# Attention with a gated feed-forward block on one core: the second weight block is converted during attention, the magnitude of the next raw words is taken ahead of the sigmoid, and scale chains move

## The chip, the core and the metric

The kernel runs on one core of a Trainium2 chip. Its time is the device time of one execution in microseconds (us); three timed runs of the kernel before gave 844.94, 845.30 and 847.82 us, median 845.3. Engines are named as in the profile: PE (matrix products), PEld (its weight loads), DVE (VectorE), ACT (ScalarE), POOL (GpSimd), SP (the queue from which most DMAs are issued; ACT and POOL issue some too).

## The reference

```python
# q, k, v: (4, 12, 448, 64); w_pre, w_post: (12, 12)
scores = scale * q @ k^T
scores = einsum('bhij,hg->bgij', scores, w_pre)      # heads mixed before the softmax
attn = softmax(scores, axis=-1)
attn = einsum('bhij,hg->bgij', attn, w_post)         # heads mixed after it
x = (attn @ v), heads side by side                   # 1792 tokens x 768
xn = x / sqrt(mean(x * x) + 1e-6) * rms_g
g, val = xn @ w_gate, xn @ w_val                     # 768 -> 1536 each
out = (g * sigmoid(g) * val) @ w_out                 # 1536 -> 768
```

The three feed-forward weights arrive as 64-bit floating point numbers; the kernel turns each into 32-bit ones by bit operations, then into a pair of fp16 tiles (a high part and a remainder).

## The kernel before, in words

**Attention.** Each of the four batches is cut into four chunks of 120 query rows (the last is shorter), and a chunk into 6, 6, 6 or 5 steps: 92 steps in all, numbered t. A step runs on every engine in turn: PE makes scores of a later chunk (`qk`), mixes heads (`sp`), and of the step before mixes again (`pm`) and multiplies with v (`av`); DVE takes the row maximum (`nm`, L193), copies (`st` L158, `at_all` L240), and makes reciprocals (`t`, `rp`); ACT takes the exponential; POOL scales the second mixing matrix (`wn`). Every engine works off its own list in order. What else stands in a step is put there by tables: `jobs_at[t]` at the head of step t, `last_at[t]` at its end. `first_w` is such a job: it converts the weights of the feed-forward block 0 in four pieces of 384 columns, seven steps a piece, one instruction a step on DVE for the first five, then a store to DRAM (`wf`) and a sum of magnitudes on ACT. `fetch_w` loads a piece. The chains (`first_w_ops`, `x_scale_ops`) find one power-of-two scale from such sums: some 12 tiny DVE instructions each, two or more a step, all through one small tile `square`.

**Feed-forward.** There are 12 blocks f of 128 gate and 128 value columns, and in each the four batches b. For one (f, b) PE makes 36 products of 128x448 (`pg`, then `pv`; `both` L703 to L705 in the first row, `product` L711 to L713 later), and `swiglu` follows on DVE (`sg` L755, `u` L758), ACT (the sigmoid form `Silu`, L756) and POOL (L759). The product tiles are six PSUM tiles, three pairs. Block 0 is done in `first_row`, block 1 to 11 in the loop after it, then comes the product with w_out (`po`, 756 products).

**Converting a block.** A block has two halves of 768 columns (gate, value); `load_w` gives each three steps: `fetch` (a 768 KB DMA into `wraw`, two buffers), `begin` (ACT: the magnitude of the upper raw words, L561), `half` (DVE: four instructions L535 to L538, which need that magnitude) with its tail (ACT: sum of magnitudes, L576). `even` then runs a scale chain on DVE and writes the fp16 pair: `wh` on ACT (L929), `wl` on DVE (L933). In `convert` the magnitude stands right before the four DVE instructions. In blocks f = 2, 3, 5, 6, 8, 9 two halves of w_out are converted beside the next block's (`queue_out`); in f = 4, 7, 10 `scale_out` runs one more chain and scales four tiles on ACT.

**First row.** `first_row` converts block 1 from raw words: two loads on the ACT queue, one half ahead of the scale chain of batch 3 (`x_scale_ops(3)`, L637 to L639) and of its `x_split` (hi on ACT L673, lo on DVE L674, two of six lo on POOL L671), one after `swiglu` of batch 1, then `even(1)` with its chain. `last_rms(0)` sums columns (`pss`, L323) and ends in the tile `d`, which `spread(3)` (`psy`, L373) needs on PE after the first product of block 1.

Of the kernel before, what the change touches and what calls it, by code (L numbers as in the profile page):

```python
# [10 lines left out]
I32 = mybir.dt.int32  # L11
# [38 lines left out]
def attention_moe(ctx: ExitStack, tc, q, k, v, wpre, wpost, mask, ident, wgv, wo, rms_g, out):  # L50
# [5 lines left out]

    const = pool(ctx, "const")
    dram = ctx.enter_context(tc.tile_pool(name="dram", bufs=1, space=bass.MemoryType.DRAM))
    wf = [dram.tile([128, KT * 128], F32, name=f"wf{p}") for p in range(2)]
    xd = [dram.tile([128, KT, SP_], F32, name=f"xd{b}") for b in range(B)]  # L60
    td = [[dram.tile([128, KT, S], F32, name=f"td{i}_{g}") for g in range(2)] for i in range(7)]

# [334 lines left out]
    def job(t, f, *a):  # L397
        jobs_at[t].append((f, *a))

    for n in range(NCHUNK):  # L400
        b, c = divmod(n, NC)
        if n > 2:
            for i in range(2):
                job(6 * n - 16 + 3 * i, load_q, n, 3 * i, 3, nc.sync)
        for hp in range(H // 2):
            if n == 0:
                job(5 + 2 * hp, load_v, 0, heads_of(0)[hp])
        if n == 4:
            for i in range(4 * 7):
                job(first[n] + 4 + i, lambda i: first_w(i), i)  # L410
            for p in range(4):
                job(first[n] + 7 * p, lambda p: fetch_w(p), p)
    for t, todo_ in enumerate(list(qk_at)):
        for n, hp in todo_:
            if n % NC == NC - 1 and n + 1 < NCHUNK:
# [12 lines left out]
            op()  # L428

    chain(16, lambda: gain_ops(), 2)  # L430
    chain(first[4] + 34, lambda: first_w_ops(), 2)
    for b in range(B - 1):
        t = first[NC * b + NC + 2] + (5 if b < B - 2 else 3)
        for i in range(17):
# [150 lines left out]
    def w_pair(pl):  # L585
        return [pl.tile([128, 2 * FT, 128], F16, name=f"w{n}", tag=f"w{n}")[:, :FT] for n in "hl"]
# [29 lines left out]
            op()  # L616
        return o[:, 1:2], o[:, 2:3]

    stats = const.tile([128, 72], F32, name="stats")
    g_scale, w_scale = stats[:, 52:], stats[:, 0:20]  # L620

    def gain_ops():
        o = g_scale[:, 4:7]
# [2 lines left out]
            lambda: nc.vector.tensor_scalar(gain, g_sb, o[:, 1:2], None, ALU.mult)  # L626
        ]

    def first_w_ops():
        unit[0] = w_scale[:, 18:19]  # L630
        return largest(w_scale, 4) + power(w_scale[:, 16:19], 2, g_scale[:, 6:7])

    def x_scale_ops(b):
        t = stats[:, 20 + 13 * (b % 2) :][:, :13] if b < 2 else const.tile([128, 13], F32, name=f"stat{b}")
        o, sc = t[:, 4:7], t[:, 7:13]
        scale_x[b] = sc, o[:, 2:3]
        first_ = lambda: nc.vector.tensor_reduce(t[:, :1], sums[b][:, :S], AX.X, ALU.max)  # L637
        return [first_] + largest(t, 1, X_LEAST, X_MOST) + power(o, -59, None, 24) + [
            lambda: nc.vector.tensor_scalar(sc, g_scale[:, 8:14], o[:, 1:2], None, ALU.mult)  # L639
        ]  # L640
# [88 lines left out]

    def fetch_w(p):  # L730
        raw = conv["raw", p] = pq.tile([128, 384, 2], I32, name="wraw", tag="wraw", bufs=3)
        src = wgv[0, :, 3 * p : 3 * p + 3].rearrange("p a f -> p (a f)").bitcast(I32)
        nc.sync.dma_start(raw.rearrange("p n t -> p (n t)"), src)

    def first_w(i):

        p, i = divmod(i, 7)
        if i < 5:
            if i == 0:
                conv["t"] = pq.tile([128, 2, 384], I32, name="wac", tag="wraw", bufs=3)  # L740
                conv[p] = to_f32(conv.pop(("raw", p)), *(conv["t"][:, j] for j in range(2)))
            conv[p][i]()
        elif i == 5:
            nc.sync.dma_start(wf[p // 2][:, (p % 2) * 384 : (p % 2) * 384 + 384], conv["t"][:, 1].bitcast(F32))
            junk = conv["t"].bitcast(F32)
            nc.scalar.activation(junk[:, 0], junk[:, 1], AF.Abs, scale=2.0 ** -12, accum_out=w_scale[:, p : p + 1])

    stores, first_ps, todo = [], [], []

# [39 lines left out]
    def start_b():  # L789
# [11 lines left out]
        def w_split(p):  # L801
            hi, lo = (t[:, 3 * p : 3 * p + 3] for t in w[0])
            f = raws.pop(("w", p)).rearrange("p (a f) -> p a f", f=128)
            up = w_scale[:, 17:18]
            nc.scalar.activation(hi, f, AF.Copy, scale=up)
            nc.vector.scalar_tensor_tensor(lo, f, up, hi, ALU.mult, ALU.subtract)

# [50 lines left out]
    def part_b(ps_p):  # L858
# [41 lines left out]
        def mix(o, x, y, op=ALU.subtract):  # L900
            nc.gpsimd.tensor_tensor(o, x, y, op)

        def fetch(eng=nc.sync):
            while work and len(fetched) < 2:
                fetched.append(work.pop(0))
                fetched[-1][0].fetch(fetched[-1][1], eng)

        def convert(f):
            if fetched and fetched[0][2] <= f:
                half, p, _ = fetched.pop(0)  # L910
                half.begin(p)
                return lambda: half(p)
            return lambda: lambda: None

        aged = []

# [38 lines left out]

        def first_row():

            queue(1)
            fetch(nc.scalar)
            for b in range(B - 1):  # L960
                spread(b)
            for b in range(1, B):
                first_ps.append([ps_p.tile([128, S], F32, name=n, tag="p") for n in ("pg", "pv")])
            for kk in range(KT):
                both(first_ps[1], w[0], xs[1], kk)
            swiglu(0, 0, *first_ps[0])
            raw3 = b_pools["narrow"].tile([128, 2 * KT, S], F32, name="raw3", tag="xn01")
            for p in range(3):
                nc.sync.dma_start(raw3[:, 2 * p : 2 * p + 2], xd[3][:, 2 * p : 2 * p + 2, :S])
            raws.update({(3, kk): raw3[:, kk] for kk in range(KT)})  # L970
            while todo:
                ahead()
                _, (f, *a), *_ = todo.pop(0)
                f(*a)
            for kk in range(KT):
                both(first_ps[2], w[0], xs[2], kk)
            convert(0)()()
            for op in x_scale_ops(3):
                op()
            for kk in range(KT):  # L980
                x_split(3, kk, nc.gpsimd if kk % 3 == 1 else nc.vector)
            swiglu(1, 0, *first_ps[1])
            convert(0)()()
            for kk in range(KT):
                both(first_ps[3], w[0], xs[3], kk)
            low = even(1)
            low(0)
            low(1)
            swiglu(2, 0, *first_ps[2])
            last_rms(0)  # L990
            small.extend(const.tile([128, SP_], F32, name=n, tag="sum", bufs=2) for n in ("small", "junk"))
# [11 lines left out]

        first_row()
        for f in range(1, FT - 1):
            queue(f + 1)
            if f in OUT_AT:
                queue_out(OUT_AT[f], f)
        for f in range(1, FT):
            for b in range(B):  # L1010
# [8 lines left out]
                even_next = f < FT - 1  # L1019
                product(pg, (hi[:, :KT], lo[:, :KT]), x)  # L1020
                product(pv, (hi[:, KT:], lo[:, KT:]), x)
                second = convert(f)
                if even_next and b == 2:
                    low = even(f + 1)
                if even_next and b == 3:
                    low(1)
                count()
                tail = second()
                if even_next and b == 2:
                    low(0)  # L1030
                if f == FT - 1:
# [5 lines left out]
                    h_load(3)  # L1037
                swiglu(b, f, pg, pv)
                tail()
                if f in SCALE_AT and b:  # L1040
                    for i in ((0, 1), (2,), (3,))[b - 1]:
                        scale_out(SCALE_AT[f], i)
                if f == 1 and b == 0:
                    last_rms(1)
                if f == FT - 1:
# [134 lines left out]
```

## Time and profile before

| what | value |
|---|---|
| median of three timed runs | 845.3 us |
| the profiled execution: device time, span | 850.1 us, 848.1 us |
| PE busy | 803.2 us, 95% |
| DVE, ACT, POOL busy | 615.1 us 73%, 509.4 us 60%, 343.7 us 41% |
| attention, up to the first product of batch 1 | 0 to 362.4 us |
| first row, up to block 1 | 362.4 to 392.4 us |
| blocks 1 to 11 | 392.4 to 701.3 us |
| product with w_out, then the last stores | 701.3 to 848.1 us |

The profiled execution is 4.8 us longer than the median. Its busy times are those of a whole run; what matters for the change is where PE stands still, since PE is busy in all but 5% of the span. A bracket at the end of a row of the timeline gives the engine's idle time before that instruction and what ended it. PE's rows overlap: a product of 448 columns is shown as 0.35 us, and the next begins 0.19 us after it. `PEclk` is the granted share of PE's clock: 1.00 is 2.4 GHz, 0.50 is 1.2 GHz.

### The profile page before, as it was taken

Reading aid. Unit: us, or ns where it says so; the run is one execution under the profiler, and the core shown is the slowest. Engines: PE = TensorE matmul, PEld = TensorE weight load, DVE = VectorE, ACT = ScalarE, POOL = GpSimd, SP = SyncE. Lnnn points to the kernel's source line nnn. Section 1 sums busy time; section 2 is a strip of 40 time slices with the busy share of each in tenths; the row PEclk is TensorE's granted clock in tenths of the full one; section 3 lists DMA queues with packets and bytes.
Section 4 is the critical chain, followed back from the end, with each engine's and each line's share of the span. In section 5 each row is a group of like instructions: output and inputs, shape, how many; then the busy total and the mean of one; then the engine's idle time right before and its main releaser. Section 6 shows DMA issues by size and latency. Waiting matters only on the chain.

```text
span 848.1 us, 27070 instructions
## 1 busy us (share of the span) xinstructions
PE 803.2 (95%) x10900; PEld 490.3 (58%) x10900; DVE 615.1 (73%) x1303; ACT 509.4 (60%) x1129; POOL 343.7 (41%) x469
## 2 busy tenths in 40 slices
PE   6998998999899999896999999999999999999998
PEld 2566777767777777643555555554554455555554
DVE  5776887787787767778687878787878776547661
ACT  3676777577767776763535354445353556869850
POOL 8112443354335346841442423324334357462210
PEclk9999999999999999998999999999999999999999
DMA  7677778666855654561545553644456246466641
GB/s 218 193 227 222 218 208 234 194 201 187 222 172 181 200 173 134 177 211 37 183 129 157 165 151 102 206 142 152 134 157 203 80 155 201 112 215 174 189 137 66
DMA packets 81087, 144.58 MB, mean 170 GB/s; under 512 B 10383, under 2 KB 72493, under 8 KB 80963
## 3 DMA queue, kind: packets, MB, share of 16 engines
q1 hardware_dynamic: 79166, 138.45, 54.9%
q0 software_dynamic: 832, 2.06, 1.0%
q10 hardware_dynamic: 965, 2.34, 0.8%
q8 instruction: 86, 1.41, 0.7%
q14 instruction: 38, 0.31, 0.1%
HBM read 72.04 MB, written 31.21 MB: 122 GB/s over the span
## 4 chain that ended last, share of the span: by engine, by line
PE 73%; DVE 12%; ACT 5%; issue 4%; DMA 2%; POOL 2%; ACTq 0%; SPq 0%; DVEq 0%; POOLq 0%
PE pm L227 10%; PE qk L138 9%; PE sp L186 8%; PE av L271 8%; PE po L711 6%; PE po L713 6%; PE po L712 6%; PE pg L713 4%; PE pg L711 3%; PE pg L712 3%; PE pv L712 3%; PE pv L711 3%; PE pv L713 3%; DVE sg L755 1%; DMA td<-keep 1%
## 5 line engine op out<-in xcount | busy, mean ns | idle before, releaser
L200 ACT ACTIVATE e<-sp,nm 128x448 f32<-128x448 f32 x180 | 114.2, 637 | 91.4 <-DVE nm L193 88.2
L186 PE MATMUL sp<-r,wk_pre 64*64 64x448 f32 x720 | 163.8, 542 | 3.8 <-issue 2.7
L138 PE MATMUL qk<-k,q 64*64 64x448 f32 x768 | 153.2, 557 | 7.7 <-DMA q<-in_q 4.2
L193 DVE TENSOR_REDUCE nm<-sp 128x1 f32<-128x448 f32 x180 | 111.0, 621 | 49.9 <-PE sp L186 25.2
L227 PEld LDWEIGHTS pm<-wn,e 60*64 60x64 f32 x5152 | 109.6, 134 | 47.9 <-POOL wn L212 25.2
L212 POOL TENSOR_SCALAR wn<-wk,rp 128x60 f32<-128x60 f32 x180 | 57.4, 333 | 192.7 <-DVE rp L209 127.7
L227 PE MATMUL pm<-wn,e 60*64 60x60 f32 x5152 | 109.9, 220 | 14.5 <-issue 11.5
L711 PE MATMUL pg<-x,wh 128*128 128x448 f16 x264 | 94.7, 359 | 9.2 <-ACT wh L929 9.2
L759 POOL TENSOR_TENSOR sg<-sg,u 128x448 f32<-128x448 f32 x36 | 43.9, 1220 | 145.2 <-ACT sg L756 135.5
L756 ACT ACTIVATE sg<-sg,unit 128x448 f32<-128x448 f32 x44 | 29.3, 667 | 121.0 <-DVE sg L755 121.0
L271 PE MATMUL av<-at_all,v 64*64 64x240 f32 (+4 forms) x1728 | 95.7, 321 | 3.1 <-issue 3.1
L713 PE MATMUL pg<-x,wl 128*128 128x448 f16 x264 | 94.4, 358 | 1.7 <-DVE wl L933 1.6
L712 PE MATMUL pg<-x,wh 128*128 128x448 f16 x264 | 94.5, 358 | 0.0
L711 PE MATMUL pv<-x,wh 128*128 128x448 f16 x264 | 93.0, 352 | 0.0
L712 PE MATMUL pv<-x,wh 128*128 128x448 f16 x264 | 93.0, 352 | 0.0
L713 PE MATMUL pv<-x,wl 128*128 128x448 f16 x264 | 93.0, 352 | 0.0
L713 PE MATMUL po<-h,fac 128*128 128x448 f16 x252 | 88.8, 352 | 0.0
L711 PE MATMUL po<-h,fac 128*128 128x448 f16 x252 | 88.8, 352 | 0.0
L712 PE MATMUL po<-h,fac 128*128 128x448 f16 x252 | 88.8, 352 | 0.0
L711 PEld LDWEIGHTS <-wh 128*128 128x128 f16 x528 | 51.9, 98 | 58.5 <-ACT wh L929 10.1
L713 PEld LDWEIGHTS <-wl 128*128 128x128 f16 x528 | 52.0, 98 | 52.5 <-DVE wl L933 3.8
L712 PEld LDWEIGHTS <-wh 128*128 128x128 f16 x528 | 52.0, 98 | 48.9 <-issue 1.6
(182 smaller groups left out, 1583.5 us busy)
## 6 DMA issues: line engine op xcount, KB each, us to landing
r<-st SPq DMA_DIRECT2D x117, 210.0 KB
hraw<-td SPq DMA_DIRECT2D x84, 224.0 KB
wraw<-in_wgv SPq DMA_DIRECT2D x20, 768.0 KB
td<-keep SPq DMA_DIRECT2D x48, 224.0 KB
wraw<-in_wo SPq DMA_DIRECT2D x12, 768.0 KB
r<-st SPq DMA_DIRECT2D x44, 175.0 KB
v<-in_v SPq DMA_DIRECT2D x24, 256.0 KB
k<-in_k SPq DMA_DIRECT2D x24, 224.0 KB
```

Of the source, the lines that this page charges most:

```text
L138: nc.tensor.matmul(ps[j][m, :S], qt[n][sl, hp, m], kt[n // NC, hp][sl], start=True, stop=True)
L186: nc.tensor.matmul(o, wk_pre[sl], rt[n][sl, 2 * p + v_], start=True, stop=True)
L193: nc.vector.tensor_reduce(t, ps[:, :S], AX.X, ALU.max, negate=True)
L200: nc.scalar.activation(e, ps[:, :S], AF.Exp, bias=nmx.pop((n, p, u)), accum_out=sm[n, p][:, u : u + 1])
L212: nc.gpsimd.tensor_scalar(wn[n, p][:, u], wk, r[:, u : u + 1], 1.0, ALU.mult, ALU.mult)
L227: nc.tensor.matmul(o[:, :, at_], e[u_][sl, j : j + JT], w_, start=True, stop=True)
L271: nc.tensor.matmul(x, vt[b, hp][sl, j, c_], a, start=(c_ == 0), stop=(c_ == JC - 1))
L711: nc.tensor.matmul(ps, a, xh[:, kk], start=(kk == 0), stop=False)
L712: nc.tensor.matmul(ps, a, xl_[:, kk], start=False, stop=False)
L713: nc.tensor.matmul(ps, a2, xh[:, kk], start=False, stop=(kk == KT - 1))
L756: nc.scalar.activation(sg, sg, AF.Silu, scale=unit[f])
L759: nc.gpsimd.tensor_tensor(h, sg, u, ALU.mult)
```

## The change

1. `first_w` and `fetch_w` now cover eight pieces, those of block 0 and of block 1 (`ROWS[p // 4]`): the four steps' lead of the load is kept, the conversions start four steps sooner (step 23) and run to step 78 instead of 54. Two more DRAM tiles `wf` hold the result.
2. The chain of block 0 starts at step 52 instead of 57; a second chain for block 1 runs from step 79, three instructions a step.
3. `first_row` no longer converts block 1 from raw words. It loads two finished 384 KB tiles on the ACT queue, writes `wh` (ACT) and `wl` (DVE) from them after the last split of batch 2, and only then runs `swiglu` of batch 0. The six lo parts of batch 3 are all on DVE. The loads of block 2 are issued ahead of these splits, and the first half of block 2 is converted after `swiglu` of batch 1.
4. In the loop `begin` is split from `convert`: the magnitude of the next half is issued after this half's four DVE instructions are listed and ahead of this iteration's `swiglu`, so it is one iteration early; a second `fetch` stands there too.
5. `scale_out` runs one stage in each of b = 0 to 3, where it had two stages in b = 1 and none in b = 0.
6. The scale tiles of batches 2 and 3 lie in columns of `stats` instead of tiles of their own.

```diff
-            for i in range(4 * 7):
-                job(first[n] + 4 + i, lambda i: first_w(i), i)
-            for p in range(4):
-                job(first[n] + 7 * p, lambda p: fetch_w(p), p)
+            for i in range(8 * 7):
+                job(first[n] + i, lambda i: first_w(i), i)
+            for p in range(8):
+                job(first[n] - 4 + 7 * p, lambda p: fetch_w(p), p)
...
-    chain(first[4] + 34, lambda: first_w_ops(), 2)
+    chain(first[4] + 29, lambda: first_w_ops(0), 2)
+    chain(first[4] + 56, lambda: first_w_ops(1), 3)
...
+        def begin(f):
+            if fetched and fetched[0][2] <= f and not begun:
+                begun.append(fetched.pop(0))
+                begun[0][0].begin(begun[0][1])
+
         def convert(f):
-            if fetched and fetched[0][2] <= f:
-                half, p, _ = fetched.pop(0)
-                half.begin(p)
-                return lambda: half(p)
-            return lambda: lambda: None
+            begin(f)
+            if begun:
+                half, p, _ = begun.pop()
+                return half(p)
+            return lambda: None
...
-            queue(1)
-            fetch(nc.scalar)
+            w[1] = w_pair(b_pools["w2b"])
+            w1 = [b_pools["wr"].tile([128, KT * 128], I32, name="wc", tag="wc", bufs=2).bitcast(F32) for _ in range(2)]
+            for p in range(2):
+                nc.scalar.dma_start(w1[p], wf[2 + p])
+            queue(2)
...
-            swiglu(0, 0, *first_ps[0])
...
+            up = w_scale[1][:, 17:18]
+            for p, c in enumerate(w1):
+                hi, lo = (t[:, KT * p : KT * p + KT] for t in w[1])
+                c = c.rearrange("p (a f) -> p a f", f=128)
+                nc.scalar.activation(hi, c, AF.Copy, scale=up)
+                nc.vector.scalar_tensor_tensor(lo, c, up, hi, ALU.mult, ALU.subtract)
+            swiglu(0, 0, *first_ps[0])
             for kk in range(KT):
                 both(first_ps[2], w[0], xs[2], kk)
-            convert(0)()()
             for op in x_scale_ops(3):
                 op()
+            fetch()
             for kk in range(KT):
-                x_split(3, kk, nc.gpsimd if kk % 3 == 1 else nc.vector)
+                x_split(3, kk, nc.vector)
+            begin(1)
             swiglu(1, 0, *first_ps[1])
-            convert(0)()()
+            convert(1)()
             for kk in range(KT):
                 both(first_ps[3], w[0], xs[3], kk)
-            low = even(1)
-            low(0)
-            low(1)
             swiglu(2, 0, *first_ps[2])
...
-                second = convert(f)
                 if even_next and b == 2:
                     low = even(f + 1)
                 if even_next and b == 3:
                     low(1)
                 count()
-                tail = second()
+                tail = convert(f)
+                fetch()
+                begin(f + (b == 3))
...
-                if f in SCALE_AT and b:
-                    for i in ((0, 1), (2,), (3,))[b - 1]:
-                        scale_out(SCALE_AT[f], i)
+                if f in SCALE_AT:
+                    scale_out(SCALE_AT[f], b)
```

Three places show what stands where. The first is DVE in the first row of the feed-forward part of the kernel before, from the splits of batch 3 (`x_7910<-raw`) to the `wl` of block 1; `ry_7968` belongs to batch 1, `wc` and `wraw` to a half of weights, `wsum` and `unit` to the scale chain (its middle rows, of the form shown, are left out):

```order
L674 SCALAR_TENSOR_TENSOR x_7910<-raw_8022,stat_8074,x_7910 128x448 x4
L755 TENSOR_TENSOR sg<-pg,ry_7968 128x448
L758 SCALAR_TENSOR_TENSOR u<-pv,stats,ry_7968 128x448
L535 TENSOR_SCALAR wc<-wc 128x768
L536 TENSOR_SCALAR wc<-wc 128x768
L537 SCALAR_TENSOR_TENSOR wc<-wraw,wc 128x768
L538 SCALAR_TENSOR_TENSOR wc<-wraw,wc 128x768
L593 COPY wsum<-wsum 64x2
...
L611 COPY unit<-unit 64x2
L933 SCALAR_TENSOR_TENSOR wl<-wc,unit,wh 128x768 x2
```

The same engine and place in the changed kernel, from the last splits of batch 2 (`x_7963<-xr`); `ry_8019` belongs to batch 0, `ry_8023` to batch 1:

```order
L675 SCALAR_TENSOR_TENSOR x_7963<-xr,stats,x_7963 128x448 x6
L990 SCALAR_TENSOR_TENSOR wl<-wc,stats,wh 128x768 x2
L756 TENSOR_TENSOR sg<-pg,ry_8019 128x448
L759 SCALAR_TENSOR_TENSOR u<-pv,stats,ry_8019 128x448
L638 TENSOR_REDUCE stats<-sum_7076 128x1
...
L640 TENSOR_SCALAR stats<-stats 128x6
L675 SCALAR_TENSOR_TENSOR x_7963<-raw_8071,stats,x_7963 128x448 x6
L756 TENSOR_TENSOR sg<-pg,ry_8023 128x448
L759 SCALAR_TENSOR_TENSOR u<-pv,stats,ry_8023 128x448
L536 TENSOR_SCALAR wc<-wc 128x768
```

The `wl` of block 1 moved from behind eight conversion instructions and two chains to ahead of everything that concerns batch 3, and the conversion that is left (now block 2's) stands behind the splits of batch 3.

ACT in the loop, kernel before, b = 1 to 2 of block 6 (`wo_8610<-wraw` is the magnitude of a half of w_out, `sg` the sigmoid, L719 the magnitudes of finished tiles):

```order
L756 ACTIVATE sg<-sg,unit 128x448
L576 ACTIVATE wh,wsum<-wc 128x768
L561 ACTIVATE wo_8610<-wraw 128x768
L929 ACTIVATE wh<-wc,unit 128x768 x2
L719 ACTIVATE junk,small<-sg 128x448
L756 ACTIVATE sg<-sg,unit 128x448
```

The same place in the changed kernel:

```order
L562 ACTIVATE wo_8585<-wraw 128x768
L757 ACTIVATE sg<-sg,unit 128x448
L577 ACTIVATE wh,wsum<-wc 128x768
L937 ACTIVATE wh<-wc,unit 128x768 x2
L720 ACTIVATE junk,small<-sg 128x448
L562 ACTIVATE wo_8585<-wraw 128x768
L757 ACTIVATE sg<-sg,unit 128x448
```

The magnitude that DVE needs in b = 2 stood behind the sigmoid of b = 1; now it stands in front of it, and the one that b = 3 needs stands in front of the sigmoid of b = 2.

DVE in attention, changed kernel, around step 66, where the chain of batch 1 ran alone before (`wac<-wac` is the added conversion; the other rows are those of every step and two of the chain):

```order
L599 TENSOR_SCALAR square<-stats 1x32
L600 STREAM_TRANSPOSE square<-square 32x32
L537 TENSOR_SCALAR wac<-wac 128x384
L193 TENSOR_REDUCE nm<-sp 128x1 x2
L158 COPY st<-qk 128x448
L240 COPY at_all<-pm 128x84x5
L207 TENSOR_SCALAR t<-s 128x2
L209 RECIPROCAL rp<-t 128x2
L608 TENSOR_SCALAR stats<-square 32x1
```

In the kernel before the row `wac<-wac` is absent there; it now stands ahead of the row maximum of the step.

## Rows read from the trace of the kernel before

**Rows 1.** PE timeline, first row to w_out: start, us, instruction, [idle before, what ended it]

```profile
375.81 0.35 PE L705 MATMUL pv<-x,wl 128*128 128x448 f16 x1
376.77 0.35 PE L703 MATMUL pg<-x,wh 128*128 128x448 f16 x1 [0.61 <-ACT x L673]
...
384.53 0.85 PE L323 MATMUL pss<-ones,sum 128*112 128x1 f32 x8
392.35 0.56 PE L711 MATMUL pg<-x,wh 128*128 128x448 f16 x1 [6.96 <-ACT wh L929]
...
401.37 0.92 PE L373 MATMUL psy<-d,ones 112*128 112x448 f32 x2
...
422.56 0.35 PE L711 MATMUL pg<-x,wh 128*128 128x448 f16 x1
...
558.76 0.35 PE L711 MATMUL pg<-x,wh 128*128 128x448 f16 x1
...
586.95 0.36 PE L711 MATMUL pg<-x,wh 128*128 128x448 f16 x1 [0.79 <-ACT wh L929]
...
671.69 0.36 PE L711 MATMUL pg<-x,wh 128*128 128x448 f16 x1 [1.44 <-ACT wh L929]
...
701.30 0.35 PE L711 MATMUL po<-h,fac 128*128 128x448 f16 x1
```

**Rows 2.** DVE timeline, first row, same columns

```profile
372.90 0.61 DVE L637 TENSOR_REDUCE stat<-sum 128x1 f32<-128x448 f32 x1
...
375.79 0.23 DVE L639 TENSOR_SCALAR stat<-stats,stat 128x6 f32<-128x6 f32 x1
376.75 0.69 DVE L674 SCALAR_TENSOR_TENSOR x<-raw,stat,x 128x448 f16<-128x448 f32 x1 [0.74 <-ACT x L673]
378.48 1.60 DVE L674 SCALAR_TENSOR_TENSOR x<-raw,stat,x 128x448 f16<-128x448 f32 x2 [1.04 <-ACT x L673]
...
383.85 0.79 DVE L535 TENSOR_SCALAR wc<-wc 128x768 f32<-128x768 f32 x1 [0.96 <-ACT wc L561]
...
392.33 1.95 DVE L933 SCALAR_TENSOR_TENSOR wl<-wc,unit,wh 128x768 f16<-128x768 f32 x2 [1.00 <-ACT wh L929]
...
398.58 0.62 DVE L363 TENSOR_TENSOR d<-eye,y 112x448 f32<-112x448 f32 x1
```

**Rows 3.** POOL timeline, first row

```profile
377.96 1.03 POOL L671 TENSOR_TENSOR x<-raw,x 128x448 f16<-128x448 f32 x1 [8.51 <-ACT x L670]
```

**Rows 4.** ACT timeline, first row

```profile
368.68 0.89 ACT L561 ACTIVATE wc<-wraw 128x768 f32<-128x768 f32 x1
```

**Rows 5.** Windows: length, each engine's busy us (count), PEclk, DMA share, GB/s

```profile
390.00:396.00 6.00, 3.52 (x10) 1.18 (x11) 4.72 (x15) 2.92 (x4) 0.41 (x1) 0.50 0.26 100
531.50:558.80 27.30, 27.30 (x146) 14.13 (x145) 21.17 (x37) 11.81 (x24) 9.50 (x8) 1.00 0.61 187
670.00:677.00 7.00, 5.06 (x18) 1.98 (x17) 5.24 (x14) 5.11 (x11) 1.75 (x1) 0.76 0.21 74
```

**Rows 6.** Waits of the whole span: us in total, times, longest

```profile
DVE wc L535 <- ACT wc L561: 34.8, 20, 2.8
...
PE pm L227 <- issue: 11.5, 13, 2.1
```

**Rows 7.** Windows in attention, columns as in rows 5

```profile
214.60:313.70 99.10, 92.61 (x2504) 74.05 (x2499) 75.09 (x197) 71.40 (x189) 41.49 (x94) 1.00 0.66 191
113.00:214.60 101.60, 94.35 (x2498) 74.88 (x2493) 79.39 (x205) 73.70 (x200) 42.96 (x94) 0.98 0.71 207
166.30:181.90 15.60, 15.55 (x406) 10.36 (x402) 14.25 (x43) 11.91 (x32) 10.61 (x26) 1.00 0.64 188
249.70:264.90 15.20, 15.20 (x430) 11.98 (x426) 13.08 (x39) 11.48 (x30) 9.26 (x26) 1.00 0.55 168
```

**Rows 8.** Instructions on the tile `wac`: shortest, median, longest ns, first and last start

```profile
L538 DVE SCALAR_TENSOR_TENSOR wac<-wraw,wac x4: 534/538/540, 124.3 to 203.4; 128x384 int32<-128x384 int32 x4
```

**Rows 9.** DMA queues: packets, MB, share of 16 engines

```profile
q8 instruction: 86, 1.41, 0.7%
```

More of the change, by code (lines that the diff above doesn't have):

```diff
@@ L58, in attention_moe @@
     dram = ctx.enter_context(tc.tile_pool(name="dram", bufs=1, space=bass.MemoryType.DRAM))
-    wf = [dram.tile([128, KT * 128], F32, name=f"wf{p}") for p in range(2)]
+    wf = [dram.tile([128, KT * 128], F32, name=f"wf{p}") for p in range(4)]
     xd = [dram.tile([128, KT, SP_], F32, name=f"xd{b}") for b in range(B)]
@@ L617, in scaled @@
         return o[:, 1:2], o[:, 2:3]
-    stats = const.tile([128, 72], F32, name="stats")
-    g_scale, w_scale = stats[:, 52:], stats[:, 0:20]
+    stats = const.tile([128, 92], F32, name="stats")
+    g_scale, w_scale = stats[:, 52:], [stats[:, 0:20], stats[:, 72:92]]
     def gain_ops():
@@ L627, in gain_ops, with first_w_ops @@
         ]
-    def first_w_ops():
-        unit[0] = w_scale[:, 18:19]
-        return largest(w_scale, 4) + power(w_scale[:, 16:19], 2, g_scale[:, 6:7])
+    def first_w_ops(f):
+        unit[f] = w_scale[f][:, 18:19]
+        return largest(w_scale[f], 4) + power(w_scale[f][:, 16:19], 2, g_scale[:, 6:7])
     def x_scale_ops(b):
-        t = stats[:, 20 + 13 * (b % 2) :][:, :13] if b < 2 else const.tile([128, 13], F32, name=f"stat{b}")
+        t = stats[:, 20 + 13 * b : 33 + 13 * b] if b < 2 else w_scale[b - 2][:, :13]
         o, sc = t[:, 4:7], t[:, 7:13]
@@ L731, in fetch_w @@
         raw = conv["raw", p] = pq.tile([128, 384, 2], I32, name="wraw", tag="wraw", bufs=3)
-        src = wgv[0, :, 3 * p : 3 * p + 3].rearrange("p a f -> p (a f)").bitcast(I32)
+        src = wgv[ROWS[p // 4], :, 3 * (p % 4) : 3 * (p % 4) + 3].rearrange("p a f -> p (a f)").bitcast(I32)
         nc.sync.dma_start(raw.rearrange("p n t -> p (n t)"), src)
@@ L745, in first_w @@
             junk = conv["t"].bitcast(F32)
-            nc.scalar.activation(junk[:, 0], junk[:, 1], AF.Abs, scale=2.0 ** -12, accum_out=w_scale[:, p : p + 1])
+            nc.scalar.activation(junk[:, 0], junk[:, 1], AF.Abs, scale=2.0 ** -12, accum_out=w_scale[p // 4][:, p % 4 : p % 4 + 1])
     stores, first_ps, todo = [], [], []
@@ L803, in w_split @@
             f = raws.pop(("w", p)).rearrange("p (a f) -> p a f", f=128)
-            up = w_scale[:, 17:18]
+            up = w_scale[0][:, 17:18]
             nc.scalar.activation(hi, f, AF.Copy, scale=up)
@@ L901, in mix @@
             nc.gpsimd.tensor_tensor(o, x, y, op)
+        begun = []
         def fetch(eng=nc.sync):
@@ L1005, in part_b @@
         for f in range(1, FT - 1):
-            queue(f + 1)
+            if f > 1:
+                queue(f + 1)
             if f in OUT_AT:
```

## The prediction

> **What bounds the kernel now.** I read the page first, then PE's timeline through the second half, then what the other engines did in each hole of PE, then attention by windows. The reader is to see that PE sets the end from the first row on, and that its holes can be counted. In the loop a block takes 27.24 us: five blocks lie between 422.56 and 558.76, 136.20 us [rows 1]. That is 4 x 36 products, 0.189 us each, 6.81 us a batch, and PE is busy in all of such a block (27.30 of 27.30 [rows 5]), so in it nothing on another engine costs time. All that can be won there is time in which PE does not go at this pace:
>
> (a) Batch 3 of the first row: the last product of batch 2 starts at 375.81, so the next could start at 376.00; it starts at 376.77, and its 36 take until 384.53, 7.76 us instead of 6.81 [rows 1]. Lost: 0.77 + 0.95 = 1.72 us.
> (b) The column sums take 0.85 us from 384.53; block 1 starts at 392.35, having waited 6.96 us for `wh` [rows 1]. Lost: 7.82 - 0.85 = 6.97 us.
> (c) Block 1 takes 422.56 - 392.35 = 30.21 us, 2.97 more than the others. `psy` is some 0.75 of it and stays. The rest, 2.22, is the clock: from 390 to 396 it was granted at 0.50, 1.2 GHz, right behind the hole of (b) [rows 5].
> (d) From 558.76 to 701.30 there are again five blocks, in 142.54 us: 6.34 lost, at the starts of blocks 8, 10 and 11, where PE waits for `wh` and `wl`; around the start of block 11 the clock falls too (0.76 from 670 to 677) [rows 1, 5].
>
> Together 17.25 us. From 701.30 on PE has no hole worth naming.
>
> **The change part by part.** *Block 1 from finished tiles.* Before, `wh` of block 1 came behind a half (from 383.85, itself late by 0.96 for the magnitude on ACT), its tail, a chain, and ran just ahead of `wl` at 392.33 [rows 2]. Now its inputs are two loads and a scale that attention has left. The loads are 384 KB each in the place of 768 KB each; the first of the old ones had landed when ACT came to it at 368.68, without a wait [rows 4], so both new ones, 768 KB together, should be there by then. `wh` and `wl` are then done at about 371, more than 12 us ahead of need. (b) goes, and with the hole the low clock of (c).
>
> *What is late next there.* The scale chain of batch 3 started at 372.90 and ended at 376.02 [rows 2], behind a half of block 1. Now two `wl` (1.95 us) and a `swiglu` (1.2 us) stand in that half's place, both about as long or shorter, and the last split of batch 2 no longer waits behind the sigmoid on ACT. I let the chain end at 376.0 at the latest and 374.3 at best. The six splits then follow at 0.69 each [rows 2], PE takes one kk in 1.13 us, so at most the first is late, by 0.7. (a) gives back 1.0 to 1.7; I take 1.4. After the splits DVE has a `swiglu` (1.2), one half of block 2 (3.0 to 4.2, the 8.5 us from 383.85 to 392.33 less a chain and two waits), and what ran from 394.28 to 399.20, the `swiglu` of batch 2 and the root up to `d`, 4.9 us [rows 2]. From 376.0 with 4.8 for the splits that ends at 389.9 to 391.1; PE wants `d` at 383.7 + 6.81 = 390.5. So it is hidden, or costs 0.6. I take 0. The half waits for a raw load that is now issued only behind the loads of batch 3; ACT stands on it ahead of a sigmoid, and behind the sigmoid wait only POOL and stores.
>
> *The magnitude ahead of the sigmoid.* Twenty times DVE waited for it, 34.8 us in all [rows 6]. In a block with four conversions DVE was busy 21.17 of 27.30 us [rows 5], the six that are left being such waits. Blocks 5 and 6 both have four, so DVE falls back, and the chain of `scale_out` in block 7 and the scale of block 8 come behind it: this is (d). Issued an iteration early, the magnitude is ready when DVE comes; DVE then has 6 us of slack in 27, and the extra chain of blocks 4, 7 and 10 (some 3 us, now a batch earlier) fits. A half's raw load has one iteration, 6.81 us, from the release of its buffer. SP now waits for that release ahead of the stores of the same iteration; eight tiles of the pool behind them last for more than three iterations, so I price it at 0. Bounds: nothing of (d) comes back, or all 6.34; DVE's slack speaks for nearly all, and I take 5.7.
>
> *Attention.* Added on DVE: 20 conversion instructions, at most 0.54 us each [rows 8], and twelve tiny ones of about 0.17; on ACT four sums; on SP eight DMAs. If nothing hid them they would cost 10.8 + 2.0 = 12.8 us. Two stretches of five equal steps (chunks 7 and 11) tell more: with a chain and conversions 15.6 us, with a chain alone 15.2 [rows 7], 0.08 a step. For 28 added steps that is 2.2. The long stretches say the same: 28 steps with conversions took 101.6, the 28 after them 99.1, and the first had the low clock (0.98), worth 1.7 of these 2.5 [rows 7]. The first chain moves from 6 free steps to 6 full ones; that combination is the 15.6. I take 2.0, between 0.8 and 2.5, and keep 12.8 above and -2 below, because PE's unexplained waits (`issue`, 11.5 us [rows 6]) may fall otherwise either way.
>
> A rule speaks against these additions. Two conversion instructions of each piece have two inputs in SBUF, and POOL works 41 to 43 of each 100 us in attention [rows 7]. In the first row two splits of the same kind take 1.60 together, the first beside POOL's 1.03 from 377.96, where one alone takes 0.69 [rows 2, 3]. The Trainium skill, SBUF — State Buffer, section "Who interferes with whom", says that a DVE instruction with two SBUF inputs and a GpSimd instruction that reads SBUF exclude each other for their whole length; the trace of the first row agrees. By the rule the eight added ones could each wait about 0.35, 3 us more. But the four that ran in attention took 534 to 540 ns [rows 8], as equal as if POOL were not there, so I add nothing.
>
> *The rest.* The scale columns and the spread of `scale_out` change no count of work; DVE's chain there only starts a batch earlier.
>
> **Sum.** 1.4 + 6.9 + 2.2 + 5.7 = 16.2 gained, 2.0 paid: 14.2. The profiled execution, 850.1 us, would become 835.9. It was 4.8 longer than the median of the timed runs; the holes are waits between engines in the second half, which these runs have as well, so I take 14.2 from the median: 845.3 - 14.2 = 831.1, about 831.
>
> **Rivals.** *The fetch of instructions.* The queue `q8 instruction` moved 86 packets, 1.41 MB, and PE's `pm` waited 13 times for nothing that the profile shows, up to 2.1 us [rows 6, 9]. If these are blocks of instructions held up by data, 2.3 MB more in 28 steps of attention could bring four more, 0.9 us each, and two spells of low clock at 1.7: 7.0. Then 838. The Trainium skill, Runtime: NRT & Kernel Launch, section "Instruction fetch mechanics", says that such blocks come over a DMA queue of their own in 16 KiB pieces and that this is mostly hidden; 1.41 MB in 86 packets agrees with the size, and by the rule's "mostly hidden" nothing would be added. Against the rival: the stretch with conversions had no more time than its low clock explains.
>
> *The first row keeps part of its hole.* The raw half of block 2, or `ry` behind it, comes late, the third pair of product tiles is not free, PE waits some 3.5 us and the clock falls again (2.2): 5.7 less, 837. For: PE arrives there 9 us sooner, and the margin at `d` is under 1 us. Against: all DVE work up to there is counted above.
>
> *The magnitude was not the cause of (d).* ACT now stands on late raw loads, and DVE as before falls back in the blocks with four conversions: 5.7 less, 837. For: SP's waits move too. Against: DVE's 6 us of slack.
>
> *Slower: the step of attention follows DVE.* Every added instruction stands ahead of the row maximum, which holds the exponential, `wn` and the next `pm`. If DVE sets the step in all of the conversion steps, 12.8 us, and PE's holes bring five spells of low clock, 8.5, then 21.3 is paid for 16.2: 850. It decides from 0.58 us an added step. For: with both kinds DVE was busy 14.25 of 15.60 [rows 7]. Against: that stretch still ran at 3.12 a step.
>
> **How the numbers follow.** Forecast 0.62, fetch 0.10, first row 0.11, (d) stays 0.12, slower 0.05. The forecast's own range is 827 (all 17.25, attention -1) to 834. Two of the middle rivals together give 842 to 844. The range 826 to 840 holds the forecast and each middle rival alone. A measurement of this kernel can tell 0.5%, 4.2 us, from no change. Faster by more needs under 841.1: the forecast, and nearly all of the three middle rivals, 0.86; same 0.08, where two of these meet; slower 0.06.
>
> **What would show it.** In the changed profile block 1 starts within 1.5 us of the column sums and takes 28.0 us, with no row of clock 0.50 there; all later blocks take 27.2; the wait of DVE for the magnitude is gone from the list of waits; chunk 11 takes 15.2 to 15.6. Wrong it would be with a PE wait of over 2 us for `ry`, `d` or a product tile in blocks 1 and 2, with waits of ACT for `wraw` that DVE inherits, or with attention more than 5 us longer.

## The result: 13.8 us faster, and the profile after

| | before | changed |
|---|---|---|
| median, us (range, runs) | 845.97 (844.94 to 847.82, 4) | 832.19 (830.51 to 832.75, 4) |
| profiled execution / span, us | 850.1 / 848.1 | 832.4 / 830.6 |
| mean granted clock of PE | 0.989 | 0.998 |
| first product of batch 1 to the end, us | 485.7 | 469.3 |

The ratio is 0.9831, 95% interval [0.9808, 0.9855]: 13.8 us gained by the medians, 14.2 forecast. Three views of the changed kernel carry the reading. First PE's timeline (start, duration, instruction, and in brackets the idle time before it and what ended it); its rows answer to [rows 1], with line numbers one higher:

```profile
374.70 0.35 PE L706 MATMUL pv<-x,wl 128*128 128x448 f16 x1
375.34 0.35 PE L704 MATMUL pg<-x,wh 128*128 128x448 f16 x1 [0.28 <-ACT x L674]
376.06 0.35 PE L705 MATMUL pg<-x,wh 128*128 128x448 f16 x1 [0.37 <-DVE x L675]
...
382.68 0.85 PE L323 MATMUL pss<-ones,sum 128*112 128x1 f32 x8
383.39 0.35 PE L712 MATMUL pg<-x,wh 128*128 128x448 f16 x1
...
390.20 0.92 PE L373 MATMUL psy<-d,ones 112*128 112x448 f32 x2
390.95 0.35 PE L712 MATMUL pg<-x,wh 128*128 128x448 f16 x1
...
411.39 0.35 PE L712 MATMUL pg<-x,wh 128*128 128x448 f16 x1
...
547.59 0.35 PE L712 MATMUL pg<-x,wh 128*128 128x448 f16 x1
...
574.83 0.35 PE L712 MATMUL pg<-x,wh 128*128 128x448 f16 x1
...
656.54 0.35 PE L712 MATMUL pg<-x,wh 128*128 128x448 f16 x1
...
683.78 0.35 PE L712 MATMUL po<-h,fac 128*128 128x448 f16 x1
```

Block 1 follows the column sums at 383.39 with no wait, where 6.96 us stood before, and takes 28.00 us to 411.39. The last five blocks take 683.78 - 547.59 = 136.19 us, 27.24 each, and their first products have no bracket any more. Only batch 3 still waits, 0.28 and 0.37.

Windows of the changed kernel (start:end, length, busy time of PE, PEld, DVE, ACT and POOL, granted clock, DMA share, GB/s), against [rows 5] and [rows 7]:

```profile
163.40:181.90 18.50, 16.05 (x444) 12.49 (x438) 13.98 (x42) 12.46 (x32) 9.79 (x26) 1.00 0.68 207
245.00:264.70 19.70, 19.11 (x483) 14.29 (x483) 16.86 (x52) 11.62 (x30) 11.27 (x27) 1.00 0.54 168
382.00:390.00 8.00, 8.00 (x48) 4.53 (x47) 7.54 (x18) 4.20 (x10) 2.11 (x2) 1.00 0.32 98
390.00:396.00 6.00, 6.00 (x31) 3.12 (x30) 4.41 (x8) 2.04 (x5) 1.14 (x1) 1.00 0.39 73
520.30:547.60 27.30, 27.30 (x147) 14.10 (x145) 25.32 (x40) 14.19 (x28) 11.88 (x8) 1.00 0.69 201
```

From 390 to 396 the granted clock is 1.00 where it was 0.50. DVE is busy 25.32 of block 6's 27.30 us, not 21.17: work stands where the waits were (point 5 says which). The first two rows, chunk 7 and six steps around chunk 11, are read under point 6 below.

The list of waits of the changed kernel (who, for whom: us in total, times, longest), against [rows 6]:

```profile
PE pm L227 <- issue: 9.0, 11, 2.3
ACT wc L562 <- DMA wraw<-in_wgv: 12.4, 9, 2.3
ACT wo L562 <- DMA wraw<-in_wo: 8.9, 6, 2.0
```

The row of DVE waiting for the magnitude, 34.8 us before, is not in it. ACT now stands on late raw loads instead, and PE inherits nothing of it: all blocks from the second on take 27.24 us.

### The profile page after: what moved, and what is told of

Its sections match the earlier page's. It is cut to its first block, busy times and chain, and to the rows that moved or that the text cites. A ratio compares the mean times of both kernels' runs of the same rounds, so it can differ in the third digit from the quotient of the medians.

```text
span 830.6 us, 27090 instructions
## 1 busy us (share of the span) xinstructions
PE 799.2 (96%) x10900; PEld 487.4 (59%) x10900; DVE 632.2 (76%) x1317; ACT 507.8 (61%) x1129; POOL 353.0 (42%) x467
## 3 DMA queue, kind: packets, MB, share of 16 engines
q8 instruction: 86, 1.41, 0.7%
## 4 chain that ended last, share of the span: by engine, by line
PE 88%; DMA 4%; issue 3%; DVE 2%; ACT 1%; POOL 1%; SPq 0%; ACTq 0%; DVEq 0%; POOLq 0%
PE pm L227 9%; PE qk L138 9%; PE sp L186 8%; PE av L271 7%; PE pg L712 6%; PE pv L713 6%; PE pg L713 6%; PE pv L712 6%; PE pg L714 6%; PE pv L714 6%; PE po L712 6%; PE po L714 6%; PE po L713 6%; DMA k<-in_k 1%; DMA xr<-xd 1%
## 5 line engine op out<-in xcount | busy, mean ns | idle before, releaser
L212 POOL TENSOR_SCALAR wn<-wk,rp 128x60 f32<-128x60 f32 x180 | 59.9, 346 | 188.8 <-DVE rp L209 125.8
L760 POOL TENSOR_TENSOR sg<-sg,u 128x448 f32<-128x448 f32 x36 | 47.1, 1308 | 149.4 <-ACT sg L757 105.2
L712 PE MATMUL pg<-x,wh 128*128 128x448 f16 x264 | 93.0, 352 | 0.0
L713 PE MATMUL pg<-x,wh 128*128 128x448 f16 x264 | 93.0, 352 | 0.0
L271 PEld LDWEIGHTS av<-at_all,v 64*64 64x64 f32 x1728 | 70.8, 133 | 8.0 <-issue 7.7
```

What stands on the lines that cost most here:

```text
L212: nc.gpsimd.tensor_scalar(wn[n, p][:, u], wk, r[:, u : u + 1], 1.0, ALU.mult, ALU.mult)
L271: nc.tensor.matmul(x, vt[b, hp][sl, j, c_], a, start=(c_ == 0), stop=(c_ == JC - 1))
L712: nc.tensor.matmul(ps, a, xh[:, kk], start=(kk == 0), stop=False)
L713: nc.tensor.matmul(ps, a, xl_[:, kk], start=False, stop=False)
L760: nc.gpsimd.tensor_tensor(h, sg, u, ALU.mult)
```

## The experiments

Each kernel was timed in five rounds beside the kernel before, whose median was 845.7 to 846.2 in the three groups. "Second half" is from the first product of batch 1 to the end, in the profile; "attention" is the time ahead of it. The ratio compares runs side by side and is not the quotient of two medians; a gain in us below is worked out from the ratio unless the text says "by the medians".

| run | median, us | ratio to before [95%] | attention | second half |
|---|---|---|---|---|
| changed kernel again | 833.99 | 0.9866 [0.9831, 0.9901] | 364.7 | 469.2 |
| attention part alone | 849.8 | 1.0041 [1.0021, 1.006] | 362.1 | 484.7 |
| and first row, old loop | 837.88 | 0.9921 [0.9891, 0.9952] | 359.4 | 475.0 |
| early magnitude alone | 840.1 | 0.9938 [0.9908, 0.9968] | 358.2 | 480.5 |
| old stages of `scale_out` | 836.03 | 0.9889 [0.9851, 0.9926] | 365.3 | 469.2 |
| conversion twice | 835.51 | 0.9904 [0.9866, 0.9942] | 362.5 | 469.5 |
| more DMA | 836.64 | 0.9912 [0.9878, 0.9947] | 364.2 | 469.1 |
| last `wn` on DVE | 833.5 | 0.9868 [0.9831, 0.9905] | 363.9 | 469.1 |
| before, with the added DMA | 848.67 | 1.0023 [0.9998, 1.0048] | 360.8 | 486.8 |
| before, conversion twice | 846.56 | 1.0006 [0.9978, 1.0035] | 355.6 | 485.1 |
| before, a copy | 846.54 | 1.001 [0.9982, 1.0038] | 362.4 | 486.8 |

The two last columns say how to read all of them: the second half repeats within 0.4 us in every kernel that has the new first row and the early magnitude (469.1 to 469.5), while attention scatters over almost 10 us between profiles, whatever was added to it. Most of that scatter is PE's waits in it: 22.0 us in the shortest attention (355.6), 32.1 and 31.6 in the two longest, and without its waits attention takes 331.6 to 336.4 us in all thirteen profiles.

**The changed kernel again.**

> The changed kernel once more, as the yardstick for the other runs. Both theories: about 13.8 us under the kernel before, the result already known, 12 to 16.

Measured 11.3 us under before here (11.9 by the medians), just short of the 12 expected, and 13.8 by the medians in the runs above; both intervals hold 12.5 to 14.

**The attention part alone** (changes 1, 2 and 6; the first row still converts block 1 from raw words):

```diff
+            for i in range(8 * 7):
+                job(first[n] + i, lambda i: first_w(i), i)
...
+    chain(first[4] + 56, lambda: first_w_ops(1), 3)
```

> Only the work in attention is added (eight pieces, the second chain, the moved first chain); the feed-forward part is the kernel before's, which converts block 1 from raw words again, so what attention prepared is not used. Holes theory (the gain is PE's holes (a) to (d), attention pays about 2): 2 us slower than before, 0 to 3.5, with holes (a) to (d) as before. Rival one (attention pays nothing and the holes are worth less in timed runs): within 0.7 us of before. Rival two (DVE sets the attention step): 6 to 13 us slower.

It costs 3.5 us [1.8, 5.1], timed, at the upper edge of what was expected. The waits of this kernel that the other parts are to take away all stand:

```profile
DVE wc L536 <- ACT wc L562: 34.0, 19, 2.8
...
PE pg L712 <- ACT wh L930: 8.6, 3, 6.9
```

Block 1 starts 15.56 us after batch 3 (8.05 in the changed kernel) and takes 30.95. Blocks 7 to 11 lose 4.0 us here, not the 6.3 of before: block 11 takes 27.92, not 29.61. PE waits about as long for `wh` at its start (1.41 here, 1.44 there), but the granted clock stays at 1.00 behind it. The first 27.9 us of block 11, before and here:

```profile
671.69:699.59 27.90, 27.40 (x135) 13.61 (x136) 21.02 (x41) 16.41 (x31) 14.97 (x12) 0.94 0.44 136
```

```profile
672.08:699.98 27.90, 27.40 (x144) 14.02 (x145) 20.95 (x44) 16.23 (x30) 14.70 (x11) 1.00 0.44 134
```

Of the six profiles with the old loop, the clock falls to 0.50 there in four and stays up in two (this one and "before, conversion twice"). So 1.7 of the 6.34 us of (d) is clock that not every execution pays.

**Attention and first row, with the old loop** (the stages of `scale_out` are put back too):

```diff
+                begin(f)
...
                 tail = convert(f)
-                fetch()
-                begin(f + (b == 3))
...
-                if f in SCALE_AT:
-                    scale_out(SCALE_AT[f], b)
+                if f in SCALE_AT and b:
+                    for i in ((0, 1), (2,), (3,))[b - 1]:
+                        scale_out(SCALE_AT[f], i)
```

> The attention part and the first row of the change, but in the loop the magnitude stands right before the four DVE instructions and the stages of scale_out as before. Holes theory: holes (a) to (c), 10.9 in the profile, are gone and (d), some 6, stays: 8 us under before (6.5 to 9.5), PE still waits for wh at the starts of blocks 8 and 11. Rival (DVE fell back in blocks 5 and 6 only since block 1 came late, so the first row alone closes (d)): as fast as the whole change, 13 to 14 under before.

From the run before to this one the ratio falls by 0.0120: 10.2 us for the first row (give or take 3), where 1.4 + 6.9 + 2.2 = 10.5 were forecast. Block 1 takes 27.99, but blocks 7 to 11 take 27.98, 27.93, 27.24, 29.45 and 29.61: without the early magnitude and the spread stages the whole of (d), 6.0 us, stays. The waits of this kernel, and PE's timeline at the starts of blocks 8 and 11 in it:

```profile
DVE wc L536 <- ACT wc L562: 32.0, 17, 2.8
```

```profile
573.28 0.36 PE L712 MATMUL pg<-x,wh 128*128 128x448 f16 x1 [0.58 <-ACT wh L937]
...
657.90 0.36 PE L712 MATMUL pg<-x,wh 128*128 128x448 f16 x1 [1.40 <-ACT wh L937]
```

**The early magnitude alone**, in the kernel before:

```diff
-                second = convert(f)
...
-                tail = second()
+                tail = convert(f)
+                fetch()
+                begin(f + (b == 3))
```

> Only the loop's early magnitude and second fetch; attention, first row and the stages of scale_out as before. Holes theory: (d) goes and (a) to (c) stay: 5.7 us under before, 4 to 6.5. Rival (DVE's lag comes from the count of its instructions, not from waiting for the magnitude): within 1 us of before, PE waits for wh at blocks 8 and 11 as before.

It gains 5.2 us [2.7, 7.8]; 5.7 were forecast for (d). Blocks 2 to 11 all take 27.24. The first row is as before: its waits and the window behind the hole in this kernel are

```profile
ACT wc L561 <- DMA wraw<-in_wgv: 11.9, 7, 2.3
...
ACT wo L561 <- DMA wraw<-in_wo: 9.0, 6, 2.9
...
PE pg L711 <- ACT wh L936: 6.9, 1, 6.9
```

```profile
384.00:395.00 11.00, 6.43 (x19) 2.46 (x20) 8.24 (x30) 6.58 (x13) 1.17 (x1) 0.53 0.23 71
```

So (d) hangs on the magnitude, issued early with its second fetch, and on nothing in the first row, and the clock of block 1 (0.53 here, 31.04 us for the block) on the hole ahead of it and on nothing in the loop. The waits of ACT for raw words are about those of the changed kernel and cost no block anything.

**Old stages of `scale_out`**, in the changed kernel:

```diff
-                if f in SCALE_AT:
-                    scale_out(SCALE_AT[f], b)
+                if f in SCALE_AT and b:
+                    for i in ((0, 1), (2,), (3,))[b - 1]:
+                        scale_out(SCALE_AT[f], i)
```

> The changed kernel with scale_out's stages where they were: two in b = 1, one each in b = 2 and 3. Holes theory (the magnitude's wait is the cause of (d), the stages are not): as fast as the changed kernel, within 1 us, 12.5 to 15 under before. Rival (the spread of the stages closes (d)): 3 to 6 us slower than the changed kernel, PE waits at blocks 8 and 11.

All blocks take 27.24 again, the second half 469.2. The earlier stages are worth nothing here. Timed, the run missed its expectation: 9.4 us under before, not 12.5 to 15. Since the second half is the same, the 2 us between the two medians should lie in attention, which this edit doesn't touch; they are inside the intervals.

**Conversion twice** in the changed kernel: every conversion instruction of attention is issued a second time:

```diff
             conv[p][i]()
+            conv[p][i]()
```

> The changed kernel with each of the 40 conversion instructions in attention issued twice in a row (the second writes the same again): some 16.5 us more of DVE work in steps 23 to 78. Holes theory, 0.08 us a step: 2 to 6 us slower than the changed kernel. Rival (DVE sets the attention step): 12 to 17 us slower than the changed kernel, no faster than before.

Forty more DVE instructions, 16.5 us of DVE work, cost 1.5 us by the medians and 3.2 by the ratios, give or take 4.4. If DVE set the step, as the slower rival had it, it would have been near 16.

**More DMA** in the changed kernel: eight more copies of 384 KB within DRAM, one beside each load of the added pieces.

```diff
+                nc.sync.dma_start(more[p], src)
```

> The changed kernel with one more 384 KB copy from DRAM to DRAM beside each of the eight loads of pieces, 6 MB moved (read and written) that nothing waits for, more than twice what the change adds. Holes theory: DMA has room, 0 to 2 us slower than the changed kernel. Rival (blocks of instructions held up by data make PE's unexplained waits): PE's waits named issue grow by 5 us or more in the profile and the time by 5 to 15.

2.6 us above the changed kernel by the medians and 3.9 by the ratios, give or take 4.1: more than the 0 to 2 expected, less than the rival's 5 to 15, and the time alone decides for neither. PE's holes in attention that end with `issue` came to 19.1 us in 21 pieces, against 21.4 in 23 in the changed kernel run again and 14.3 in 16 in its first profile: no growth by 5.

**The last chunk's `wn` on DVE** in the changed kernel, to take POOL out of the chain at the end of attention:

```diff
+            if n == NCHUNK - 1:
+                nc.vector.tensor_scalar(wn[n, p][:, u], wk, r[:, u : u + 1], None, ALU.mult)
```

> The changed kernel with wn of the last chunk (steps 87 to 91) on DVE instead of POOL. In the changed kernel's profile PE waits there for wn three times, 0.66, 0.79 and 1.23 us, while POOL works off sums. Theory: these go, 1.5 to 2.7 us under the changed kernel, a version faster than both. Rival (DVE's splits there come later by what POOL gives up, and PE meets them at the first row): within 0.7 us of the changed kernel.

A tie (0.9868 against 0.9866): a miss, no faster version. PE's three waits for POOL at the end of attention (0.66, 0.79 and 1.23 us in the changed kernel) became three for DVE (0.54, 0.49 and 0.93) and longer ones for ACT (0.36, 0.59 and 0.77).

**The kernel before with one load of the attention part at a time**, and a copy of it as the yardstick. The first adds four copies of 384 KB in the steps in which the change adds loads, the second issues the 20 conversion instructions of block 0 twice:

```diff
+                job(first[n] + 28 + 7 * p, lambda p: more_dma(p), p)
```

> The kernel before with four copies of 384 KB from DRAM to DRAM on the SP queue in the steps where the change loads the pieces of block 1; nothing waits for them, no engine gets work. The added work in attention cost 3.5 us when it ran alone. If DMA (blocks of instructions held up, loads of scores behind the copies) is its cause: 2 to 4 us slower than before. If it is the added instructions: within 1 us of before.

```diff
             conv[p][i]()
+            conv[p][i]()
```

> The kernel before with each of the 20 conversion instructions on DVE issued twice in a row, in the same steps 27 to 54; no DMA is added. If the added DVE instructions are the cause of the 3.5 us: 2 to 4 us slower than before (0.08 us a step gives 2.2). If DMA is the cause: within 1 us of before. If DVE sets the step: 8 us slower.

> The kernel before under another name, as the measure of what these comparisons can tell: ratio 1 within 0.002. In its profile the holes (a) to (d) should be those of the first profile within 1 us, while attention may differ by some us, as it did between profiles of kernels with the same attention.

The DMA alone: +1.9 us [-0.2, 4.1]. The DVE work alone: +0.5 [-1.9, 3.0]. The copy: +0.8 [-1.5, 3.2], and it must be 0; its holes are those of the first profile within 1 us. Neither load is told from nothing, nor from its half of 3.5. This is inconclusive. The profiles don't settle it either: attention averages 361.0 us in the three of the old attention without a load and 362.8 in the six of the new one, but each group spreads over 4 to 6 us.

## Why the prediction was right, point by point

1. *(a), batch 3.* Forecast 1.4, measured 0.74: mis-sized by half, and under the 1.0 to 1.7 that I gave. PE could have started at 374.70 + 0.19 = 374.89 and started at 375.34, and its 36 products then took 7.34 to the sums instead of 6.81. 0.45 + 0.53 = 0.98 is still lost. DVE's timeline in the changed kernel shows why (answers to [rows 2]):

```profile
367.31 2.16 DVE L990 SCALAR_TENSOR_TENSOR wl<-wc,stats,wh 128x768 f16<-128x768 f32 x2 [0.45 <-ACT wh L989]
...
370.51 0.61 DVE L638 TENSOR_REDUCE stats<-sum 128x1 f32<-128x448 f32 x1
...
372.15 1.13 DVE L599 TENSOR_SCALAR square<-stats 1x32 f32<-1x32 f32 x1
...
374.35 0.23 DVE L640 TENSOR_SCALAR stats<-stats 128x6 f32<-128x6 f32 x1
...
375.32 3.66 DVE L675 SCALAR_TENSOR_TENSOR x<-raw,stats,x 128x448 f16<-128x448 f32 x6 [0.74 <-ACT x L674]
...
380.03 0.55 DVE L536 TENSOR_SCALAR wc<-wc 128x768 f32<-128x768 f32 x1
...
389.02 0.62 DVE L363 TENSOR_TENSOR d<-eye,y 112x448 f32<-112x448 f32 x1
...
395.31 0.62 DVE L756 TENSOR_TENSOR sg<-pg,ry 128x448 f32<-128x448 f32 x1 [1.49 <-ACT ry L375]
```

   The chain ended at 374.58, 0.31 ahead of PE's need; before, it ended at 376.02, 0.02 behind it. Against PE's need it came only 0.33 earlier, near the late end of my bounds, and I had taken more than their middle: the two `wl` took 2.16 after a wait of 0.45 for `wh`, and one instruction of the chain took 1.13 us (0.17 in the extra chain of block 7). Behind the chain ACT's hi part of the first split still costs 0.74, as before [rows 2]. What else came back, 0.42, is in the splits behind it, 0.61 each and all on DVE. This is one pair of profiles: over batches 2 and 3 together the other five with the old first row lose 1.7 to 2.4 us, the other six with the new one 0.6 to 1.1.

2. *(b), the wait ahead of block 1.* Forecast 6.9, measured 383.39 - 382.68 = 0.71 against 7.82: 7.1. `wl` of block 1 ended at 369.47 (367.31 + 2.16), 13.9 us ahead of need.

3. *(c), the clock.* Forecast 2.2, measured 30.21 - 28.00 = 2.2. In the other kernels that keep the hole block 1 took 30.5 to 31.05, so the hole costs 2.5 to 3.1 there: the term is at its low end in the profile that I read. The difference goes with how long the clock stays low: in all six profiles it falls to 0.50 inside the hole, and it is back at 1.00 about 4 us into block 1 in the profile that I read, and almost 6 us into it where the block takes 31.04 and 31.05.

4. *`d` and the root behind it.* Ready at 389.64, PE's turn at 390.20: hidden, with the 0.6 us of margin that the early end of the forecast had. The 1.49 us that DVE waited for `ry` was no wait of PE. The rival "the first row keeps part of its hole" falls.

5. *(d), the magnitude.* Forecast 5.7, measured 6.34 in the profile and 5.2 timed alone; 1.7 of the 6.34 is clock that comes and goes (see "The attention part alone"). The cause is shown from both sides: without it (and without the spread stages, which are worth nothing) the five blocks lose 6.0, with it alone nothing. "The magnitude was not the cause" falls. One step of the argument was wrong all the same: DVE did not have "6 us of slack in 27". The window that I read held 37 instructions of a DVE that was falling behind, which is less than a block's list. One whole pass over the list, four conversions and all that goes with them, from a conversion to the same one a block later, is this before (from the first half of w_out in block 6) and in the changed kernel (from block 6's first `wc`), DVE being the third busy time:

```profile
532.37:561.68 29.31, 29.31 (x157) 15.16 (x156) 23.18 (x39) 13.27 (x26) 10.21 (x9) 1.00 0.62 190
```

```profile
523.48:550.08 26.60, 26.60 (x143) 13.73 (x141) 24.65 (x40) 13.77 (x27) 11.88 (x8) 1.00 0.71 206
```

   Before, a pass took 29.31 us, 23.18 of work and the rest waits, so DVE fell back 2.07 us in such a block; now it takes 26.60, under PE's 27.24. The slack is 27.24 - 23.18 = 4.06 by the work of before, and 27.24 - 24.65 = 2.59 by that of now: the same instructions cost 1.47 more, because five of them instead of three run long beside POOL's work. DVE and then POOL in block 6 of the changed kernel:

```profile
524.06 1.37 DVE L537 TENSOR_SCALAR wc<-wc 128x768 int32<-128x768 int32 x1
525.47 1.77 DVE L538 SCALAR_TENSOR_TENSOR wc<-wraw,wc 128x768 int32<-128x768 int32 x1
527.28 1.77 DVE L539 SCALAR_TENSOR_TENSOR wc<-wraw,wc 128x768 int32<-128x768 int32 x1
...
532.09 0.96 DVE L538 SCALAR_TENSOR_TENSOR wc<-wraw,wc 128x768 int32<-128x768 int32 x1
...
539.64 0.56 DVE L537 TENSOR_SCALAR wo<-wo 128x768 int32<-128x768 int32 x1
```

```profile
525.10 1.33 POOL L768 TENSOR_TENSOR keep<-sg,keep 128x448 f32<-128x448 f32 x1
526.50 1.73 POOL L768 TENSOR_TENSOR keep<-keep 128x448 f32<-128x448 f32 x1
528.20 1.85 POOL L768 TENSOR_TENSOR u<-sg,keep 128x448 f32<-128x448 f32 x1
```

   L538 takes 0.96 where POOL is idle and 1.77 beside it, L537 0.56 and 1.37. What was read as 6 us of slack is 2.6, and it sufficed.

6. *Attention.* Forecast +2.0, between 0.8 and 2.5; the attention part alone costs 3.5 [1.8, 5.1]. The term was under-sized and its inner bounds too narrow, though the outer ones (-2 to 12.8) held. The step that failed is the reading of 0.08 us a step out of two single stretches of 15.6 and 15.2 us. The forecast check on chunk 11 was missed: the six steps around it took 19.70, 3.28 each instead of 3.12, and chunk 7 took 18.50 instead of 15.60, PE idle 2.45 of it, at a clock of 1.00. Such waits of PE fall in other places in every profile; a difference of 0.4 between two stretches was below what one profile can tell. That attention was 1.1 shorter in this profile than in that of before (361.3 to 362.4) is the same scatter. The slower rival is out: conversions issued twice cost a tenth to a fifth of their DVE time, under half of it at the end of the interval.

7. *The fetch of instructions.* The queue still moved 1.41 MB in 86 packets. More data did not add PE waits that end with `issue`, and the 838 that this rival asked for was not met, so it is not borne out; the time of the run with more DMA doesn't exclude a part of it. What these waits are stays open.

8. *The lock.* In the first row and in the loop DVE and POOL hold each other up, as the Trainium skill, SBUF — State Buffer, section "Who interferes with whom", has it, and the rows of point 5 agree. They show the same for the instruction with one SBUF input. In attention it was priced at nothing. The conversions of the changed kernel there (count, duration min/median/max, first and last start):

```profile
L538 DVE SCALAR_TENSOR_TENSOR wac<-wraw,wac x8: 504/538/546, 107.5 to 282.6; 128x384 int32<-128x384 int32 x8
L539 DVE SCALAR_TENSOR_TENSOR wac<-wraw,wac x8: 539/540/646, 110.6 to 287.1; 128x384 int32<-128x384 int32 x8
```

   One of sixteen was 0.1 us longer: nothing on DVE, as forecast. But I was wrong to read this "as if POOL were not there": the conversion mostly starts first, some 0.25 us ahead of POOL's `wn`, and POOL pays. A pair of `wn` takes 0.60 us without a conversion beside it and 0.75 to 1.03 beside a two-input one. POOL's time in `wn` over attention grows with the number of conversion instructions: 20 (before), 40 (before with each twice), 40 (changed) and 80 (changed with each twice):

```profile
0.00:345.00 345.00, 56.66 (x179) 0.99 0.68 197
```

```profile
0.00:345.00 345.00, 61.05 (x180) 1.00 0.68 199
```

```profile
0.00:345.00 345.00, 59.34 (x180) 1.00 0.70 204
```

```profile
0.00:345.00 345.00, 65.30 (x179) 1.00 0.70 204
```

   PE's own waits for `wn` were 2.6 to 2.7 us in three of these profiles, those of before, of the changed kernel and of the changed kernel with each conversion twice; so PE shows nothing of this.

The sum by parts: 0.74 + 7.11 + 2.21 + 6.34 = 16.4 is the whole difference of the second halves (forecast 16.2). With 3.5 paid in attention it gives 12.9, between the 11.3 and the 13.8 measured in the two sets of runs; timed apart, +3.5 - 10.2 - 5.2 = -11.9. Part of the closeness of 832.19 to 831 is luck: attention cost more than I took, this set of runs happened to be on the good side, and the profile that I read had the low clock in block 11, which others have not. What in the added work costs the 3.5, the DMA or the DVE instructions, is left open.

## What to carry to other kernels

Where one engine sets the end, list its holes and price each by itself: four terms read so, from single waits and block lengths, came within 0.7 us each. A stretch whose own length scatters by microseconds can't price an edit of a tenth of a microsecond a step; time the edit alone, or keep the wide bounds. And read slack from one pass over an engine's list, not from a window in which it falls behind; even that is not all yours to spend, since taking waits away moves work beside other work, and it can grow, on either engine.

## What the runs showed of the hardware that was not expected

A DVE instruction with one SBUF input (L537, 768 int32 columns) grew from 0.56 to 1.37 us beside POOL, relatively more than the one with two (0.96 to 1.77). In attention it was POOL's instruction that grew, and the conversion that started first did not. After the same 7 us hole, block 1 took between 30.2 and 31.05 us as the granted clock stayed at 0.50 for 4 to 6 us of it; and behind a wait of 1.4 us for `wh` at block 11 it fell in four profiles and not in two others. What a hole costs in clock differs from one execution to the next. PE's waits for nothing that the profile shows came to 8.8 to 21.4 us of attention in different profiles, and no load that was added to DVE or DMA raised them.
